# mLSTM cell and tanh-shrink MLP on one core: partial sums added in DRAM, one early unit fewer, explicit places for the later units

## The chip, the cores and the metric

The kernel runs on one core of a Trainium2 chip. The metric is the device time of one execution in microseconds (us), as the median of several runs. The engines are PE (matrix products), DVE and ACT (elementwise work, ACT also activations), POOL and SP (both used here mostly to issue DMAs). PSUM is written by PE and read by DVE and ACT; eight banks of it are shared out by tags.

## The reference

An mLSTM cell over 4 batches, 8 heads, 768 steps and a head size of 40 gives x, and an MLP without bias follows:

```python
for t in range(S):
    m_new = np.maximum(f_gate[:, :, t] + m, i_gate[:, :, t])
    f_stab = np.exp(f_gate[:, :, t] + m - m_new)
    i_stab = np.exp(i_gate[:, :, t] - m_new)
    C = f_stab * C + i_stab * np.einsum('bhd,bhe->bhde', vt, kt)
    n = f_stab * n + i_stab * kt
    y[:, :, t] = sigmoid(o_gate[:, :, t]) * (C @ qt) / np.maximum(np.abs(n @ qt), 1.0)
x = y.transpose(0, 2, 1, 3).reshape(3072, 320)
h = x @ w_in                  # 320 x 2048
g = h - np.tanh(h)
out = g @ w_out               # 2048 x 320
```

(m is carried along, and broadcasts are left out.) All is float32.

## The kernel before, in words

**Units and groups.** The cell is computed in chunks of 128 steps. A unit is one chunk of one batch with all its heads: 24 units, n = 4 x chunk + batch, so unit n needs the state that unit n - 4 left. Two units make a group of 256 tokens for the MLP: 12 groups. The 2048 hidden columns are eight pairs of 128-column blocks. The work of a group with a pair is an up product (x by w_in, tiles ph_up), g from a polynomial (z, q on ACT, gt on DVE) and a down product (gt by w_out).

**A unit.** Loads of k, v, o and of k and q turned (kz, qz). The scores ps = q k, then P (ps by the mask of decays, on DVE or by ACT and POOL), vs (v scaled), the products of P with vs and of the old state with q (ph), then the gate: den, o and ys, which is y. The update of the state is pc. The turn of y to x (px, xT) lets the up product read it.

**Two forms of a unit.** The units below PLANNED belong to the first part: ph has the tokens on the partitions, and y is turned by PE. The later units are turned through DRAM. Their products give pT with the head's dimensions on the partitions (`block_turned`); `turn_back` writes zt with DVE and sends it by SP as h_rows and back as z_in; `gate_turned` makes den, o and two ys of it in four steps; `turn_by_store` turns ys to yt on DVE, sends it by SP as y_rows, and reads it back as xT. SP's queue is served in order. All of one unit's zt legs and y legs go through it.

**Items.** The MLP is worked off in 49 items, each a pair of (group, pair). The table `RUNS` sets the first 11: they hold groups 0 to 3 with pairs 0 to 3, and group 0 with pairs 4 to 7. Their down products for pairs 0 to 3 run plainly into a bank po of each unit, and where a run of pairs ends (`evict`), po goes into an SBUF tile `part`: the first time by a copy on ACT, after that by an add on DVE. START is the twelfth item, from which on the dense part runs: 38 items with split up products (x_thirds, w_thirds) and a down product in seven multiplications (pS), for which DVE makes the sums s. `put_together` combines the banks of a group on DVE and, for groups 0 to 3, adds `part`; POOL sends the result.

**What sets the order.** In the first part a list scheduler, `Plan`, takes the step that can start first, by engine times written into the code, and among equal ones by rank; it fills waits of PE with products whose result is unused (awake). In the dense part the code's own order is the order on each engine. An item lists its PE steps with costs, and `merge` puts other steps among them by their place within the item. `cell_slot` places the steps of two units into a slot of two items: begin of unit s and the load of unit s + 1 (by POOL) at its start, `prepare` (vs) a fifth of the way, and the four gate steps and the store of unit s - 1 in its last quarter. The unit's scores ps stand in the item where it begins and `block_turned` in the one behind.

Of the kernel before, what the change touches and what calls it, by code (L numbers as in the profile page):

```python
# [61 lines left out]
L = 128  # L62
# [26 lines left out]
def kernel(  # L89
# [76 lines left out]
    class Plan:  # L166
# [14 lines left out]

        def add(self, engine, us, step, after=(), rank=0.0, take=(), give=(), at=0.0, kb=0.0, tiles=1, hold=0.0, dense=1.0, lag=None, small=False):
# [122 lines left out]
    FIRST, SPLIT, PLANNED, TAIL = 4, 4, 9, 1  # L305
# [71 lines left out]
    def load_unit(n, names=("kz", "qz", "v", "k", "o", "q2"), queue=SP, behind=(), crossed=False):  # L377
# [3 lines left out]
        for name in names:  # L381
# [3 lines left out]
            elif name in ("kz", "qz"):  # L385
                t[name] = load.tile([128, HH, L], FP, name=name, tag=f"{name}{(n + 1) % 3 if n < PLANNED and not general else n % 2}", bufs=1)
# [568 lines left out]
    def cell_slot(s, o):  # L955


        steps, pause = [], [(0.0, lambda: None)]
        if s is not None:
            if s + 1 < NU and s + 1 not in ld:  # L960
                load_unit(s + 1, ("kz", "qz", "v", "k", "o"), G, crossed=True)
            begin(s)
        if o is None:
            return [(0.0, lambda: prepare(s))]
        steps += 5 * pause
        if s is not None:
            steps.append((0.0, lambda: prepare(s)))
        steps += 8 * pause
        gates = []
        steps.append((0.0, lambda: [gates.extend(gate_turned(o)), gates[0]()]))  # L970
        steps += [(0.0, lambda i=i: gates[i]()) for i in range(1, 4)]
        steps.append((0.0, lambda: turn_by_store(o)))
        return steps + 2 * pause


# [77 lines left out]

    def put_together(g, halves_of=False):
# [14 lines left out]
        def end():  # L1069
            V.tensor_tensor(out=ob[:, 1:3], in0=bank[2], in1=u, op=OP.add)  # L1070
            if g < FIRST:
                both = ob[:, 0:2 * GT]
                V.tensor_tensor(out=both, in0=both, in1=parts_of[g].rearrange("p t (two n) -> p (t two) n", two=2), op=OP.add)
            c, b = divmod(g * GT, B)
            rows = out.rearrange("(b c t) n -> c t b n", b=B, c=NT)[c][:, b:b + GT]
            Clock.later("sent", 2.0, lambda: G.dma_start(out=rows, in_=ob[:, 0:4].rearrange("p (t two) n -> p t (two n)", two=2)))
# [273 lines left out]
    def down(x, some, g, p, first, last, evict_at_once=True):  # L1350
# [10 lines left out]
        def evict(tt):  # L1361
            n = g * GT + tt
            if last < NP - 1:
                if first:
                    V.tensor_tensor(out=part[n], in0=po[tt], in1=part[n], op=OP.add)
                else:
                    A.copy(out=part[n], in_=po[tt])
                return
            ob = mlp.tile([128, 5, HM], FP, name="ob", tag="ob")[:, 0:2].rearrange("p two n -> p (two n)")
            if first:  # L1370
                V.tensor_tensor(out=ob, in0=po[tt], in1=part[n], op=OP.add)
            else:
                A.copy(out=ob, in_=po[tt])
            send(n, ob, 1.0)
# [42 lines left out]
    RANKS = (-1.0, -1.0, -8.2006, -8.4463, 6.0242, 2.3893, 9.5327, 2.6415, 25.6922, 13.6176, 29.7021, 7.061)  # L1417
    WEIGHTS = (0.08, -0.3563, 5.1266, 7.6972, 9.6586, 11.6503, 11.1391, 25.4848)
# [7 lines left out]
    def gates(c0, c1, rank, at, banks_of, after=()):  # L1426
# [3 lines left out]
        for step in gate_rows(c0, c1):  # L1430
            op = plan.add("V", 0.2 + long, step, [op] if op else [*after, *rows[-1:]], rank, at=at)
# [5 lines left out]
        def add(engine, us, name, after, take=None, give=None):  # L1437
# [6 lines left out]
            op = plan.add(engine, us, step, after, rank, dense=0.2, take=[(names[take], mine)] if take is not None else (), give=[(names[give[0]], mine)] if give else ())  # L1444
# [27 lines left out]
    def plan_gates(i, rank, at, banks_of):  # L1472
        c0, c1 = CHUNKS[i:i + 2]
        after = [plan.add("S", 1.6, lambda: load_gates(c0, c1), (), rank - 0.5, at=at - 4.0, kb=33 * (c1 - c0))] if c0 > 1 else []
# [7 lines left out]
    def plan_unit(n, rank):  # L1482
# [7 lines left out]
        def load(name, us, kb, after):  # L1490
            u[name] = plan.add("S", us, lambda: [load_unit(n, (name,), behind=[T.last] if n == 2 and name == "kz" else ()), arrive(n)], of(*after) + of(n - 1, name), rank + LATE.get(name, 0.0) + 2.0 * (n < 2), at=6.0 + 8.0 * (n < 2), kb=kb, small=name == "q2")
# [27 lines left out]
        u["scores"] = plan.add("T", 1.0, first_part, [u["qz"], *(of(n - 2, "second") if n in (2, 3) else [])], rank, [(bank, held), ("P", held)], tiles=2, hold=HOLD * (n // B), dense=0.4 if n else 0.6)  # L1519
        if n in BY_POOL:  # L1520
            copies = [plan.add("A", 0.55, lambda i=i: ready[1][i][0](), [u["scores"]], rank - 6.4275, give=[(bank, held)] if i else ()) for i in range(2)]
            u["mask"] = [plan.add("G", 0.9, lambda i=i: ready[1][i][1](), [copies[i]], rank + 2.098, lag=0.1) for i in range(2)]
        else:
            u["mask"] = [plan.add("V", 0.62, lambda i=i: ready[1][i](), [u["scores"]], rank - 1.673, give=[(bank, held)] if i else ())
# [3 lines left out]
        u["prep"] = plan.add("V" if alone else "A", 0.45 if alone else 1.9, lambda: prepare(n, whole=False, by_heads=not alone), [u["v"], u["scores"], *of_tokens[c]], rank, [("vs", held)])  # L1528
        u["column"] = plan.add("A", 0.2, lambda: un[n]["column"](), [u["prep"]], rank - 0.2)
        u["open"] = plan.add("A", 0.47 if n else 1.75, lambda: open_gate(n), [u["o"], u["column"] if n < 2 else u["scores"], *of_states[0], *exponentials], rank - 0.1)  # L1530
# [9 lines left out]
        for j, heads in enumerate(parts):  # L1540
            op = plan.add("T", 0.223 * len(heads) + (0.22 if c else 0.0), lambda j=j, heads=heads: second_part(j, heads),
# [3 lines left out]
        if shared:  # L1545
            steps = []
            over = plan.add("V", 0.6, lambda: [steps.extend(gate(n, in_parts=True)), steps[0]()], [op], rank - 0.2851)
            shares = plan.add("A", 1.9, lambda: steps[1](), [over, u["open"]], rank + 9.0221)
            u["gate"] = plan.add("V", 0.5, lambda: steps[2](), [shares, *of(n - 2, "turn")], rank - 7.2476, give=[("small", held)])
        else:  # L1550
            u["gate"] = plan.add("V", 1.6, lambda: gate(n), [op, u["open"], *of(n - 2, "turn")], rank, give=[("small", held)])
# [13 lines left out]
        u["turn"] = plan.add("T", 0.35, turns, [u["gate"]], rank, [("small", held_x)], dense=0.5)  # L1565
        u["x"] = plan.add("A", 0.5, lambda: keep_x(n), [u["turn"]], rank + 1.345, give=[("small", held_x)])
        late = rank + (3.0653 if c else -10.0273)
        u["update"] = plan.add("T", 0.64, updates, [u["second"], u["k"]], late, [("small", held_c)], [("vs", held)],
                               at=0.0 if c else 0.0 if n < 2 else 50.4842, dense=0.5)
        u["state"] = plan.add("V", 1.0 if c else 0.5, lambda: keep_state(n), [u["update"], *before, *of_states[c]], late, give=[("small", held_c)])  # L1570
# [3 lines left out]
    def plan_weights(p, rank, at):  # L1574
        for k, block in enumerate(blocks_of(p)):
            fetch, parts, low, power, one, sign, product = block
            held, r, buffer = {}, rank + 4.428 * k, "w64" + "ab"[k]
            op = plan.add("G", 0.6 if k else 2.2, lambda fetch=fetch: fetch(begun[-1:]), begun_in_plan[:], r, [(buffer, held)], at=FETCH.get((p, k), at), kb=655)
            op = plan.add("V", 0.8, parts, [op], r, [("w", held)])
            if p == k == 0:  # L1580
                first_parts.append(op)
            two = [plan.add("A", 0.74, step, [op], r) for step in (low, power)]
            op = plan.add("V", 0.75, one, two[:1], r)
            op = plan.add("V", 0.75, sign, [op, two[1]], r, give=[(buffer, held)])
            converted[p, k] = plan.add("V", 0.75, product, [op] + (of_tokens[NT - 1] + of_states[NT - 1] if p >= KEPT and k == 1 else []), r, give=[("w", held)])
# [3 lines left out]
    for n in range(2):  # L1589
        plan_unit(n, -1.0)  # L1590
    plan_weights(0, 0.08, 3.4)
    begun_in_plan[:] = first_parts
    for n in range(2, PLANNED):
        if n == 2 * B:
# [15 lines left out]
    def plan_item(x):  # L1610
# [17 lines left out]
        for k in range(2 * n):  # L1628
            op = plan.add("T", 0.87, lambda k=k: products(k), [op] if op else [*need, *firsts[-1:]], rank, () if op else [("up", held)])
# [7 lines left out]
        op = ups[x] = plan.add("T", 0.43 * n, rest, [op], rank, tiles=2, dense=0.7)  # L1637
# [398 lines left out]
```

## Time and profile before

| what | us |
|---|---|
| runs | 491.85, 491.89, 496.38; median 491.89 |
| profiled execution | 492.65, span 490.9 |
| first dense product on PE | 139.72 |
| DVE busy, PE busy | 405.9 (83%), 476.0 (97%) |
| ACT busy, POOL busy | 256.8 (52%), 125.1 (25%) |

The span is what the profiler sees between the first and last instruction; the rest of the time is around it. In the rows below, a line shows start or group, engine, operation, the tile that it writes, the tiles that it reads, and shapes. Nearly all instructions carry the line of a helper (L115 or L138), so they are told apart by tile names. A bracket at the end shows how long the engine was idle before, and what ended that.

### The profile page before, as it was taken

Reading aid. Unit: us, or ns where it says so; the run is one execution under the profiler, and the core shown is the slowest. Engines: PE = TensorE matmul, PEld = TensorE weight load, DVE = VectorE, ACT = ScalarE, POOL = GpSimd, SP = SyncE. Lnnn points to the kernel's source line nnn. Section 1 sums busy time; section 2 is a strip of 40 time slices with the busy share of each in tenths; the row PEclk is TensorE's granted clock in tenths of the full one; section 3 lists DMA queues with packets and bytes.
Section 4 is the critical chain, followed back from the end, with each engine's and each line's share of the span. In section 5 each row is a group of like instructions: output and inputs, shape, how many; then the busy total and the mean of one; then the engine's idle time right before and its main releaser. Section 6 shows DMA issues by size and latency. Waiting matters only on the chain.

```text
span 490.9 us, 12662 instructions
## 1 busy us (share of the span) xinstructions
PE 476.0 (97%) x4783; PEld 426.6 (87%) x4783; DVE 405.9 (83%) x918; ACT 256.8 (52%) x600; POOL 125.1 (25%) x230
## 2 busy tenths in 40 slices
PE   8999999999999998999999999999999999999994
PEld 5778888777789898889999999999999999999994
DVE  5999969999979999997996896986888878775643
ACT  4566597765375656434544445445345454455450
POOL 4523304352003250532442351342143000000000
PEclk9999999999999999999999999999999999999999
DMA  7988737341001443535444454454454532320001
GB/s 222 294 257 257 194 66 133 116 140 44 1 1 58 83 103 70 146 88 120 107 104 106 108 125 83 108 119 83 90 124 89 95 77 41 64 60 1 28 1 33
DMA packets 122625, 49.57 MB, mean 101 GB/s; under 512 B 102806, under 2 KB 114710, under 8 KB 122558
## 3 DMA queue, kind: packets, MB, share of 16 engines
q1 hardware_dynamic: 112390, 23.12, 23.7%
q0 software_dynamic: 9968, 25.25, 17.1%
q8 instruction: 40, 0.66, 0.6%
q10 hardware_dynamic: 200, 0.33, 0.2%
q14 instruction: 27, 0.22, 0.2%
HBM read 37.57 MB, written 10.81 MB: 99 GB/s over the span
## 4 chain that ended last, share of the span: by engine, by line
PE 80%; DVE 11%; DMA 4%; issue 2%; ACT 1%; POOL 1%; SPq 0%; DVEq 0%
PE ph_up L138 34%; PE pS L138 26%; PE po L138 7%; PE ph L138 3%; DVE gt L115 3%; PE ps L138 3%; PE pT L138 3%; DMA w<-in_moe_w_in 2%; PE pc L138 2%; DVE s L115 2%; DVE w_thirds L115 1%; DVE zt L115 1%; DVE x_thirds L115 1%; DVE ob L115 1%; DMA h_rows<-zt 1%
## 5 line engine op out<-in xcount | busy, mean ns | idle before, releaser
L115 ACT ACTIVATE z<-ph_up 128x512 f32<-128x512 f32 (+1 forms) x98 | 56.8, 584 | 96.1 <-PE ph_up L138 96.1
L115 ACT ACTIVATE ph_up<-ph_up 128x512 f32<-128x512 f32 x76 | 44.2, 582 | 87.0 <-PE ph_up L138 83.4
L115 DVE SCALAR_TENSOR_TENSOR gt<-ph_up,z 128x512 f32<-128x512 f32 (+1 forms) x98 | 62.8, 673 | 23.4 <-ACT z L115 23.1
L138 PE MATMUL pS<-wT,s 128*128 128x160 f32 x480 | 72.0, 299 | 0.2 <-DVE s L115 0.2
L138 PEld LDWEIGHTS pS<-wT,s 128*128 128x128 f32 x480 | 67.3, 190 | 0.6 <-DVE s L115 0.4
L115 ACT ACTIVATE q<-z,tiny 128x512 f32<-128x512 f32 (+1 forms) x98 | 65.5, 711 | 0.6
L115 DVE SCALAR_TENSOR_TENSOR gt<-q,gt 128x512 f32<-128x512 f32 (+1 forms) x98 | 63.2, 673 | 0.0
L115 POOL DMA_DIRECT2D out<-ob x11 | 8.0, 726 | 208.7 <-DVE ob L115 129.4
L138 PE MATMUL pS<-w_out,gt 128*128 128x160 f32 x320 | 58.6, 312 | 0.0
L138 PE MATMUL ph_up<-x_thirds,w_high 128*128 128x256 f32 x304 | 52.0, 293 | 4.1 <-DVE gt L115 4.1
L138 PE MATMUL ph_up<-xT,w_half 64*64 64x256 f32 (+1 forms) x624 | 53.5, 392 | 0.0
L138 PEld LDWEIGHTS pS<-w_out,gt 128*128 128x128 f32 x320 | 45.5, 189 | 4.8 <-issue 3.0
L138 PE MATMUL ph_up<-x_thirds,w_thirds 128*128 128x256 f32 x304 | 48.4, 281 | 0.6 <-DVE x_thirds L115 0.6
L138 PEld LDWEIGHTS ph_up<-x_thirds,w_high 128*128 128x128 f32 x304 | 41.6, 188 | 5.1 <-issue 3.7
L138 PE MATMUL ph_up<-thirds,w_thirds 128*128 128x256 f32 x280 | 44.1, 292 | 0.4 <-ACT ph_up L115 0.4
L138 PEld LDWEIGHTS ph_up<-x_thirds,w_thirds 128*128 128x128 f32 x304 | 41.2, 188 | 0.8 <-DVE x_thirds L115 0.8
L138 PEld LDWEIGHTS ph_up<-xT,w_half 64*64 64x64 f32 (+1 forms) x624 | 27.7, 144 | 12.7 <-issue 3.0
L138 PE MATMUL ph_up<-xT,w_in 128*128 128x256 f32 x160 | 38.3, 383 | 0.0
L138 PE MATMUL po<-w_out,gt 128*128 128x320 f32 x128 | 38.0, 441 | 0.0
L138 PEld LDWEIGHTS ph_up<-thirds,w_thirds 128*128 128x128 f32 x280 | 37.1, 189 | 0.8 <-ACT ph_up L115 0.8
L138 PEld LDWEIGHTS ph_up<-xT,w_in 128*128 128x128 f32 x160 | 29.5, 190 | 4.3
L138 PEld LDWEIGHTS po<-w_out,gt 128*128 128x128 f32 x128 | 23.2, 190 | 9.6 <-issue 0.8
(143 smaller groups left out, 862.5 us busy)
## 6 DMA issues: line engine op xcount, KB each, us to landing
w<-in_moe_w_out POOLq DMA_DIRECT2D x8, 640.0 KB, 5.8
w<-in_moe_w_in POOLq DMA_DIRECT2D x16, 256.0 KB, 4.7
h_rows<-zt SPq DMA_DIRECT2D x60, 64.0 KB
z_in<-h_rows SPq DMA_DIRECT2D x60, 64.0 KB
out<-ob POOLq DMA_DIRECT2D x11, 320.0 KB, 2.8
y_rows<-yt SPq DMA_DIRECT2D x60, 48.0 KB
xT<-y_rows SPq DMA_DIRECT2D x30, 96.0 KB
kz<-in_kT POOLq DMA_DIRECT2D x28, 80.0 KB, 2.7
```

The source lines that it names most:

```text
L115: i = method(*args, **kwargs)
L138: return cls.keep(nc.tensor.matmul(*args, **kwargs))
```

## The change

It has four parts.

1. **Parts added in DRAM.** The DVE adds into `part` and the add of `part` in `put_together` are gone. Each run's po is copied by ACT into `part` and sent by POOL to `out` (`send_group`): the first send of a group stores, every later one, that of `put_together` among them, is a DMA that adds to what lies there, with a dependency on the group's send before it. Ten such stores stand in the first part, four plain and six adding.
2. **One planned unit fewer.** PLANNED goes from 9 to 8, so unit 8 is computed in the dense form. Units 8 and 9 are both loaded by SP ahead of START.
3. **Explicit places.** `cell_slot` is gone. Unit n begins at item START + max(0, 2(n - 8) - 1); its `prepare` stands 0.45 items on, the load of unit n + 2 (by POOL) 1.7 on, the four gate steps 2.7 to 2.97 and the store 3.06 on.
4. **New order of the first part.** Every step of the plan has a name, and a table `SHIFTS` adds a number to the rank of each name; the ranks of units and weights are new too.

```diff
+        SHIFTS = {"update": -76.14, "g": -103.12, "x": 41.17, "column": 70.86, "turn": -207.65, "shared": -147.21,
...
+            rank, self.name = rank + self.SHIFTS.get(self.name, 0.0), None
...
-    FIRST, SPLIT, PLANNED, TAIL = 4, 4, 9, 1
+    FIRST, SPLIT, PLANNED, TAIL = 4, 4, 8, 1
...
+    def send_group(g, tile):
+        c, b = divmod(g * GT, B)
+        rows = out.rearrange("(b c t) n -> c t b n", b=B, c=NT)[c][:, b:b + GT]
+        i = G.dma_start(out=rows, in_=tile, **({"accum_op": OP.add} if g in stored else {}))
+        if g in stored:
+            tc.add_manual_dep(i.ins, stored[g].ins.name, SYNC, reason="order of additions")
+        stored[g] = i
...
             V.tensor_tensor(out=ob[:, 1:3], in0=bank[2], in1=u, op=OP.add)
-            if g < FIRST:
-                both = ob[:, 0:2 * GT]
-                V.tensor_tensor(out=both, in0=both, in1=parts_of[g].rearrange("p t (two n) -> p (t two) n", two=2), op=OP.add)
...
-                if first:
-                    V.tensor_tensor(out=part[n], in0=po[tt], in1=part[n], op=OP.add)
-                else:
-                    A.copy(out=part[n], in_=po[tt])
+                A.copy(out=part[n], in_=po[tt])
...
-    slots = [tuple(n if PLANNED <= n < NU else None for n in (s, s - 1)) for s in range(PLANNED, NU + 1)]
-    last = item((NG - 1) * NP) - 2.0
-    for i, slot in enumerate(slots):
-        x0, x1 = (START + (last - START) * j / len(slots) for j in (i, i + 1))
-        begins[int(x0)].append((slot, x0, x1))
+    def place(at, step):
+        work[int(at)].append((at, 0.0, step))
+
+    def gate_at(n, at):
+        gates = []
+        place(at, lambda: [gates.extend(gate_turned(n)), gates[0]()])
+        for i in range(1, 4):
+            place(at + 0.09 * i, lambda i=i: gates[i]())
+        place(at + 0.36, lambda: turn_by_store(n))
+
+    EACH = ("kz", "qz", "v", "k", "o")
+    for n in range(PLANNED, NU):
+        at = START + max(0, 2 * (n - PLANNED) - 1)
+        begins[at].append(n)
+        place(at + 0.45 * (n > PLANNED), lambda n=n: prepare(n))
+        if n + 2 < NU:
+            place(at + 1.7, lambda n=n: load_unit(n + 2, EACH, G, crossed=True))
+        gate_at(n, at + 2.7)
```

**The order on DVE in one dense period.** The rows run from the end of den (the reciprocal) to yt and what follows. Names: gt<-ph_up and gt<-q are the two steps of g, each for half an item; ys is y by its low and high dimensions; yt its turn for the store; zt belongs to the next unit; s are the sums for the down products. Before:

```order
L115 RECIPROCAL den<-den 128x8
L115 TENSOR_TENSOR o<-o,den 128x320
L115 SCALAR_TENSOR_TENSOR gt<-ph_up,z 128x512 x2
L115 TENSOR_TENSOR ys_156<-z_in,o 128x8x32
L115 TENSOR_TENSOR ys_156<-z_in,o 128x8x8
L115 STREAM_TRANSPOSE yt<-ys_156 128x256
L115 STREAM_TRANSPOSE yt<-ys_156 128x128
L115 TENSOR_TENSOR thirds<-x_thirds 128x768
L115 SCALAR_TENSOR_TENSOR gt<-q,gt 128x512
L115 STREAM_TRANSPOSE zt<-pT 128x64
```

and in the changed kernel:

```order
L115 RECIPROCAL den<-den 128x8
L115 SCALAR_TENSOR_TENSOR gt<-ph_up,z 128x512
L115 TENSOR_TENSOR o<-o,den 128x320
L115 SCALAR_TENSOR_TENSOR gt<-ph_up,z 128x512
L115 TENSOR_TENSOR ys_157<-z_in,o 128x8x32
L115 SCALAR_TENSOR_TENSOR gt<-q,gt 128x512
L115 TENSOR_TENSOR ys_157<-z_in,o 128x8x8
L115 SCALAR_TENSOR_TENSOR gt<-q,gt 128x512
L115 TENSOR_TENSOR s_3215<-gt 128x256 x2
L115 TENSOR_TENSOR s_3216<-s_3215,gt 128x256
L115 TENSOR_TENSOR s_3217<-gt,s_3216 128x256
L115 STREAM_TRANSPOSE yt<-ys_157 128x256
```

den now stands ahead of the first gt<-ph_up of an item instead of the next one's beginning, and between it and yt the whole of an item's g and sums has moved in; in every second unit thirds stands between the two ys.

**The order on POOL in the first part.** w are the fetches of weights (w_in in four pieces, w_out in one), P the masked scores that POOL makes, out the stores. Before, in the middle of the first part:

```order
L115 AFFINE_SELECT P<-P 128x512 x2
L115 DMA w_690<-in_moe_w_in 128x256
L115 DMA w_690<-in_moe_w_in 128x2x128
L115 DMA w_690<-in_moe_w_in 64x128 x2
L115 DMA w_774<-in_moe_w_in 128x256
L115 DMA w_774<-in_moe_w_in 128x2x128
L115 DMA w_774<-in_moe_w_in 64x128 x2
L115 AFFINE_SELECT P<-P 128x512 x2
L115 DMA w_951<-in_moe_w_out 128x2x320
```

and in the changed kernel:

```order
L115 DMA out<-part 128x2x320
L115 DMA w_714<-in_moe_w_out 128x2x320
L115 AFFINE_SELECT P<-P 128x512 x2
L115 DMA w_796<-in_moe_w_in 128x256
L115 DMA w_796<-in_moe_w_in 128x2x128
L115 DMA w_796<-in_moe_w_in 64x128 x2
L115 DMA out<-part 128x2x320 x2
L115 DMA w_881<-in_moe_w_out 128x2x320
```

Stores of parts now stand between the fetches: five of the ten ahead of the last fetch, five behind it. PE's rows ahead of START keep their counts except for unit 8's (ps 72 to 64, ph<-vs,P 72 to 64, ph<-state 10 and 5 to 8 and 4, pc 18 and 9 to 16 and 8, px 27 to 24) and awake (42 to 39). On ACT the last copy of po stands behind the first x_thirds of the dense part.

More of the change, by code (lines that the diff above doesn't have):

```diff
@@ L180, in __init__, with of @@
             self.tiles, self.done = 1, []
+        def of(self, name):
+            self.name = name
+            return self
+        name = None
+        SHIFTS = {"update": -76.14, "g": -103.12, "x": 41.17, "column": 70.86, "turn": -207.65, "shared": -147.21,
+                  "g_load": -260.96, "store": 132.5, "split": 51.35, "open": 92.01, "state": 54.14, "x_up": -14.25,
+                  "cube": -104.02, "fetch": 221.34, "evict": -174.94, "sums_g": -102.61, "parts": 88.45, "z": -27.79,
+                  "q": 67.28, "product": -162.48, "up": -125.33, "sums_w": 39.35, "seven": 113.81, "over": 90.23,
+                  "gates": -99.77, "pool_mask": 113.85, "mask": -9.78, "loads": 84.62, "two": 160.52, "down": 87.24,
+                  "second": -26.64, "x_cross": -316.14, "g_rows": 204.49, "sign": -118.98, "one": -105.4, "scores": -344.38,
+                  "copy": -55.99, "gate": -17.9, "x_low": -187.13, "rest": 27.76, "prep": -282.1, "share": -195.25}
         def add(self, engine, us, step, after=(), rank=0.0, take=(), give=(), at=0.0, kb=0.0, tiles=1, hold=0.0, dense=1.0, lag=None, small=False):
             self.serial += 1
+            rank, self.name = rank + self.SHIFTS.get(self.name, 0.0), None
             op = {"engine": engine, "us": us, "step": step, "after": list(after), "rank": rank, "serial": self.serial,
@@ L953, in gate_turned @@
         return [over, share, lambda: product(0), lambda: product(1)]
[L955 to L973, printed above, removed]
     gT, po = {}, {}
@@ L1430, in gates @@
         for step in gate_rows(c0, c1):
-            op = plan.add("V", 0.2 + long, step, [op] if op else [*after, *rows[-1:]], rank, at=at)
+            op = plan.of("g_rows").add("V", 0.2 + long, step, [op] if op else [*after, *rows[-1:]], rank, at=at)
         rows.append(op)
@@ L1442, in step @@
                 steps[name]()
-            op = plan.add(engine, us, step, after, rank, dense=0.2, take=[(names[take], mine)] if take is not None else (), give=[(names[give[0]], mine)] if give else ())
+            op = plan.of("gates").add(engine, us, step, after, rank, dense=0.2, take=[(names[take], mine)] if take is not None else (), give=[(names[give[0]], mine)] if give else ())
             return op if take is None else (op, (take, mine))
@@ L1768 @@
         G.memset(tile[:, H:], 0.0)
-    load_unit(PLANNED, ("kz", "qz", "v", "k", "o"), crossed=True)
+    for n in (PLANNED, PLANNED + 1):
+        load_unit(n, EACH, crossed=True)
     FIRST_B = [(PLANNED + i) % B for i in range(B)]
@@ L1787 @@
         dense, new, scored = [], [], news
-        for slot, x0, x1 in begins[x]:
-            spread_over(cell_slot(*slot), x0, x1)
-            if slot[0] is not None:
-                new.append(slot[0])
+        for n in begins[x]:
+            begin(n)
+            new.append(n)
         if x < len(items):
```

101 lines of the change are left out of this document (52 added, 49 removed).

## The prediction

> **What bounds the kernel now.** I read the table of stages first, to see which engine is full in which part, then the DVE and SP timelines of one dense period, then the waits, then the groups that the change adds and removes. The profiled execution took 492.65 us with a span of 490.9, so 1.75 us lie around the span; it is 0.76 above the median of 491.89, and every sum below is made against 492.65 and brought to the median at the end. The stages are cut at the first dense product (139.72) and at two item starts (212.48, 426.35). Columns: stretch, its length, then busy time of PE, PE weight load, DVE, ACT, POOL, clock, DMA share, GB/s.
>
> ```profile
> 20.00:139.72 119.72, 118.85 (x729) 96.33 (x728) 108.36 (x226) 78.97 (x189) 32.31 (x61) 1.00 0.50 135
> 139.72:212.48 72.76, 67.18 (x815) 62.03 (x815) 68.91 (x161) 39.23 (x95) 20.63 (x37) 1.00 0.36 81
> 212.48:426.35 213.87, 213.87 (x2682) 202.59 (x2682) 177.73 (x414) 103.29 (x239) 58.64 (x104) 1.00 0.45 98
> 426.35:490.90 64.55, 57.81 (x434) 53.56 (x433) 36.46 (x80) 25.67 (x58) 1.46 (x2) 0.99 0.09 24
> ```
>
> The first part is PE's (118.85 of 119.72 us), the early dense stretch DVE's (68.91 of 72.76), the long stretch PE's again with no idle time, at a granted clock of 1.00. By engine totals a change that takes work from DVE should do no harm. But a period of the long stretch also holds a round trip through DRAM for each unit, which no busy time shows. DVE's part of one period, in the order in which it ran:
>
> ```profile
> 286.41 0.16 DVE L115 SCALAR_TENSOR_TENSOR den<-z_in,inv 128x8 f32<-128x8 f32 x1
> 287.05 0.49 DVE L115 TENSOR_TENSOR o<-o,den 128x320 f32<-128x320 f32 x1
> 287.60 1.29 DVE L115 SCALAR_TENSOR_TENSOR gt<-ph_up,z 128x512 f32<-128x512 f32 x2
> 288.81 0.55 DVE L115 TENSOR_TENSOR ys<-z_in,o 128x256 f32<-128x256 f32 x2
> 289.39 0.64 DVE L115 STREAM_TRANSPOSE yt<-ys 128x256 f32<-128x256 f32 x2
> 291.24 0.65 DVE L115 STREAM_TRANSPOSE zt<-zt 128x448 f32<-128x448 f32 x1
> 292.98 0.75 DVE L115 TENSOR_TENSOR s<-gt 128x256 f32<-128x256 f32 x2
> 294.64 0.48 DVE L115 TENSOR_TENSOR vs<-v,crossed 128x320 f32<-128x320 f32 x1
> 299.21 1.28 DVE L115 SCALAR_TENSOR_TENSOR gt<-q,gt 128x512 f32<-128x512 f32 x2
> 305.72 0.17 DVE L115 SCALAR_TENSOR_TENSOR den<-z_in,inv 128x8 f32<-128x8 f32 x1 [1.55 <-DMA z_in<-h_rows]
> 309.12 0.92 DVE L115 TENSOR_TENSOR thirds<-x_thirds 128x768 fp32r<-128x768 f32 x1
> ```
>
> SP's queue beside it, between the first and the last unit of the stretch (the time of a row is that of issuing; a queue's next row waits for the landing it needs):
>
> ```profile
> 200.29 1.86 SPq L115 DMA_DIRECT2D y_rows<-yt  x4
> ...
> 209.30 1.90 SPq L115 DMA_DIRECT2D z_in<-h_rows  x4
> ...
> 290.06 2.46 SPq L115 DMA_DIRECT2D y_rows<-yt  x4
> 295.25 1.24 SPq L115 DMA_DIRECT2D xT<-y_rows  x2
> 296.59 2.18 SPq L115 DMA_DIRECT2D h_rows<-zt  x4
> 300.95 1.90 SPq L115 DMA_DIRECT2D z_in<-h_rows  x4
> ...
> 414.78 1.85 SPq L115 DMA_DIRECT2D y_rows<-yt  x4
> ...
> 423.13 1.90 SPq L115 DMA_DIRECT2D z_in<-h_rows  x4
> ```
>
> Read the two together as a ring. den(n) opens the gate of unit n and ends with yt(n), 3.62 us later (286.41 to 290.03). Only then SP sends y_rows(n); xT stands behind it and waits for its landing; h_rows(n+1) stands behind xT though its source zt was ready at 291.89; z_in(n+1) waits for h_rows; and den(n+1) needs z_in. That den ran at 305.72 after waiting 1.55 us for exactly this. The gap from the y_rows to the z_in issue has a mean of 9.74 us over the 13 units between 200.29 and 423.13 (9.01 for the first, 8.35 for the last, and 10.89, the longest, for the one of the DVE rows). From z_in's issue to den it is 4.21 on average over the eight units whose den waited (4.77 above). The DRAM part is thus 13.95, the ring 3.62 + 13.95 = 17.6.
>
> ```profile
> 195.85 0.16 DVE L115 SCALAR_TENSOR_TENSOR den<-z_in,inv 128x8 f32<-128x8 f32 x1
> ...
> 427.85 0.17 DVE L115 SCALAR_TENSOR_TENSOR den<-z_in,inv 128x8 f32<-128x8 f32 x1 [1.13 <-DMA z_in<-h_rows]
> ...
> DVE den L115 <- DMA z_in<-h_rows: 6.9, 8, 1.6
> ...
> PE ph_up L138 <- DVE gt L115: 4.1, 3, 1.8
> ```
>
> From den(10) at 195.85 to den(23) at 427.85 there are 13 passes in 232.0 us, 17.85 each. PE needs 18.08 for two items with a unit (rows below), so the ring and PE are level: eight dens waited, 6.9 us in all, and PE hardly felt it.
>
> ```profile
> 291.12 0.74 PE L138 MATMUL ph_up<-x_thirds,w_high 128*128 128x256 f32 x4
> ...
> 299.66 0.74 PE L138 MATMUL ph_up<-x_thirds,w_high 128*128 128x256 f32 x4
> ...
> 309.20 0.74 PE L138 MATMUL ph_up<-x_thirds,w_high 128*128 128x256 f32 x4
> ```
>
> **Explicit places (the large term).** The gate moves from +3.33 items after a begin to +2.7, and its steps are laid 0.09 of an item apart with the store of yt last, at +0.36. In the new DVE order shown ahead, den now stands before both gt<-ph_up of the item, and between den and yt stand two gt<-ph_up, o, ys, two gt<-q and the four sums s; before, it was o, two gt<-ph_up and ys. In prices of the rows above: den 0.64 (286.41 to 287.05), gt<-ph_up 2 x 0.60 (287.60 to 288.81), o 0.55, ys 0.58, gt<-q 2 x 0.64, s 1.66 (292.98 to 294.64), yt 0.64: 6.55, by the starts that overlap some 0.2 less, 6.35. In every second unit thirds (0.83) stands there too, half of it on average: 6.75. DVE has nothing to skip these with. It is idle 36 us in 214, but it runs in order, and after a den that waited everything behind it is ready.
>
> SP's order is unchanged: y_rows, xT, h_rows of the next unit, z_in. So the ring becomes 6.75 + 13.95 = 20.70 us, above PE's 18.08. What is late next is den, by about 2.6 us in every period; behind it wait both gt<-ph_up of that item, and the ph_up banks they free are those that the next item's first products write. The 13 passes cost 13 x 20.70 = 269.1; the last two carry no loads of later units and take the shortest DRAM part, 8.35 + 4.72 = 13.07, so 1.8 less: 267.3. Against 232.0 that is **+35.3**.
>
> The bounds: with 13.07 in every pass the ring is 19.82 and the term +25.7; with 15.66 (290.06 to 305.72, the slowest) it is 22.4, +59. I take the mean, since the loads now issued at +1.7 items fall into the same part of the ring as before.
>
> The Trainium skill ("DMA: Bandwidth & Descriptors", section "Anatomy of one DMA — SWDGE (gpsimd) path") gives a transfer a fixed 2.0 us and 436 GB/s beside it. Four legs in a row, of 192, 192, 256 and 256 KB here, would by that be an estimated 10.1 us, and the ring an estimated 16.9, below PE's 18.08. The trace disagrees: it measured 13.95, and that fit is for POOL's queue while these are SP's.
>
> **First part: the stores, unit 8, the new ranks.**
>
> ```profile
> L138 PE MATMUL ps<-qz,kz 40*64 40x128 f32 (+2 forms) x624 | 22.9, 251 | 0.0
> ...
> L138 PE MATMUL ph<-vs,P 128*128 128x41 f32 x144 | 18.1, 274 | 0.4 <-POOL P L115 0.4
> ...
> L138 PE MATMUL pc<-vs,k 128*64 128x41 f32 (+2 forms) x230 | 14.6, 241 | 0.0
> ...
> L138 PE MATMUL awake<-diag 128*128 128x512 bf16 x42 | 12.2, 427 | 1.1 <-DVE probe L115 1.1
> ...
> L138 PE MATMUL ph<-state,q 120*128 120x123 f32 (+1 forms) x30 | 6.0, 283 | 0.0
> ...
> L142 PE MATMUL px<-ident,ys 128*128 128x128 f32 x27 | 4.4, 278 | 0.0
> ...
> L115 DVE TENSOR_TENSOR part<-po,part 128x320 f32<-128x320 f32 x12 | 5.7, 485 | 1.9 <-PE po L138 1.8
> ...
> L115 DVE TENSOR_TENSOR ob<-ob,part 128x640 f32<-128x640 f32 x4 | 3.3, 825 | 0.1
> ...
> L115 POOL DMA_DIRECT2D out<-ob x11 | 8.0, 726 | 208.7 <-DVE ob L115 129.4 <-DVE den L115 79.4
> ```
>
> With unit 8 go from PE's first part: ps 22.9/24 = 0.95, ph<-vs,P 18.1/9 = 2.01, ph<-state 6.0/5 = 1.20, pc 14.6/20 = 0.73 (the last four units have none), the turn of x 3 x 4.4/27 = 0.49, and three awake fillers at 12.2/42 = 0.29 each: **-6.3**. All other PE counts stay. DVE loses there twelve adds of parts (12 x 0.485 = 5.8), but PE is the fuller engine, so that only widens DVE's slack and is worth nothing by itself. ACT gains twelve copies, some 5 us of the 40 it has idle in that stage. POOL gains ten stores at 0.73 us of issue, between its weight fetches. New waits stand against this: a store waits on POOL for its part's copy, and an accumulating one for the group's earlier store, with weight fetches behind it; and the last copy of po1 stands behind an x_thirds on ACT. Cover: POOL sits idle 87 of 119.72 us there, mostly for buffers. Bounds 0 and +6 (all of the relief); I take +2. START moves by **-4**, to about 135.7. What the new ranks do beyond the counts I cost at nothing, since PE has 0.9 us of idle time there to win and can lose as much as it is made to wait, inside the same +6.
>
> **Early dense stretch.** DVE bounds it. Before den(10) it now has one more z block (zt 1.4, state 0.6), one more gate (den, o, ys, yt 2.2), less two adds of parts (2 x 0.82), and a first wait of about 1: **+3.4** on the 56.13 us from 139.72 to 195.85. Unit 8's PE work fits in the 5.6 us that PE is idle there. The other two adds lie in this stretch or behind den(10), under the ring. The loads of units 8 and 9 stand on SP ahead of START and are hidden by the first part.
>
> **Tail.** den(23) stood 1.5 us into an item (427.85 against 426.35) with 8 items to come in 64.55 us, 8.07 each. Now it stands some 1.3 us before an item's end, with seven after it: 1.3 + 56.5 = 57.8 against 63.05, **-5.2**.
>
> **Sum:** -4 + 3.4 + 35.3 - 5.2 = +29.5; 492.65 + 29.5 = 522.1, and less 0.76 about **521 us** for the median.
>
> **The rivals.** (a) The ring does not bind: the DRAM part comes down to 11.3 us or less, so that den is on time. Then the passes take PE's 18.08, 13 x 0.23 = +3.0, and the sum is -4 + 3.4 + 3.0 - 5.2 = -2.8: 489, not slower. It decides where y_rows-issue to den falls by 2.6 us. The fit of the Trainium skill's page "DMA: Bandwidth & Descriptors" above speaks for it. Against it: the last unit, the shortest of the 13 by its first gap and without loads beside it, still took 13.07. (b) xT's wait is no longer in the way, and only the z trip binds: den to the freed banks 1.24, one item with a unit 9.54 (299.66 to 309.20), at whose end zt now stands, and h_rows' issue to den 9.13 (296.59 to 305.72): 19.9, 13 x 19.9 - 232.0 = +26.7 for the passes, and with the rest as above 513. SP's order, where xT stays ahead, speaks against it. (c) The chain binds and the accumulating stores also hold POOL and the weights behind them: START +4 instead of -4, 529. POOL's idle time speaks against it. (d) The first part shrinks by DVE's whole relief of about 11 us and the dense stretch loses nothing: -11 + 3.4 + 3 - 5.2 = -9.8, 482; PE's full stage speaks against it.
>
> **How the numbers follow.** The forecast has 0.60, (b) 0.13, (c) 0.08, (a) 0.13, (d) 0.06. The measurement of this kernel tells about 1% from no change, so (a) at 489 counts as the same, (d) as faster, the rest as slower: 0.06, 0.13, 0.81. The range: the ring with the shortest DRAM part gives 521 - 9.6 = 511, rival (b) 513, and if only half of the lengthening from 3.62 to 6.75 came, the ring would be 19.1 and the time about 503; toward (a) I reach to 499, and upward past (c) to 533. Outside are (a), (d) and the slowest legs in every pass.
>
> **What would show it.** Right: in the new profile den waits for z_in in nearly every period, 2 us or more each, dens stand 19.8 to 21 us apart, den to yt is 6.3 to 7.2 us, and PE waits for gt with a total of 25 to 40 us; START is at 133 to 139. Wrong: dens 18.1 apart with little wait (then (a)); yt soon after den; POOL's fetches late in the first part ((c)). The step that would fail first is that y_rows, xT, h_rows and z_in keep their 13.95 us when the ring turns more slowly and its transfers meet others.

## The result and the profile after

The changed kernel takes 546.77 us at the median against 492.04 in the same runs: a ratio of 1.107, interval 1.099 to 1.114. The direction was as forecast, the size was not: +54.7 us instead of +29, and the time lies above the range of 499 to 533. The profiled execution took 549.84 us with a span of 548.0.

The windows view of the changed kernel, cut at the same four events as in the prediction's sum (the first dense product, den(10), den(23)). Columns as before: stretch, length, busy time of PE, PE weight load, DVE, ACT, POOL, then the granted clock, DMA share, GB/s.

```profile
20.00:133.46 113.46, 113.34 (x678) 91.10 (x676) 106.74 (x211) 77.80 (x190) 34.22 (x60) 1.00 0.66 162
133.46:198.72 65.26, 58.49 (x722) 54.21 (x721) 53.96 (x131) 33.55 (x80) 23.48 (x39) 0.95 0.45 87
198.72:483.89 285.17, 247.41 (x2912) 232.33 (x2912) 192.47 (x453) 112.49 (x258) 65.41 (x114) 0.95 0.39 82
483.89:548.00 64.11, 54.64 (x398) 50.98 (x398) 35.60 (x77) 23.13 (x51) 0.71 (x1) 0.94 0.07 18
```

No engine is full in the long stretch now: PE is busy 247 of 285 us, DVE 192, and PE's granted clock has gone from 1.00 to 0.95. Against the kernel before, by stage:

| stage | before | after | difference | forecast |
|---|---|---|---|---|
| to the first dense product (START) | 139.72 | 133.46 | -6.3 | -4 |
| START to den(10) | 56.13 | 65.26 | +9.1 | +3.4 |
| 13 passes, den(10) to den(23) | 232.00 | 285.17 | +53.2 | +35.3 |
| den(23) to the end | 63.05 | 64.11 | +1.1 | -5.2 |
| span | 490.9 | 548.0 | +57.1 | +29.5 |

The waits view of the changed kernel names the place: engine, what waited, for whom, total us, times, longest.

```profile
DVE den L115 <- DMA z_in<-h_rows: 47.2, 15, 5.8
...
PE ph_up L138 <- DVE gt L115: 40.8, 14, 4.2
```

den waits in 15 of 16 units, 47.2 us against 6.9 before, and PE waits behind it for gt, 40.8 us against 4.1. One period, from the timelines of DVE, PE and SP:

```profile
356.48 0.17 DVE L115 SCALAR_TENSOR_TENSOR den<-z_in,inv 128x8 f32<-128x8 f32 x1 [3.24 <-DMA z_in<-h_rows]
...
357.96 0.68 DVE L115 SCALAR_TENSOR_TENSOR gt<-ph_up,z 128x512 f32<-128x512 f32 x1
...
361.89 0.63 DVE L115 STREAM_TRANSPOSE yt<-ys 128x256 f32<-128x256 f32 x2
...
366.67 0.65 DVE L115 STREAM_TRANSPOSE zt<-zt 128x448 f32<-128x448 f32 x1
...
377.64 0.17 DVE L115 SCALAR_TENSOR_TENSOR den<-z_in,inv 128x8 f32<-128x8 f32 x1 [3.07 <-DMA z_in<-h_rows]
```

```profile
357.79 0.71 PE L138 MATMUL ph_up<-x_thirds,w_high 128*128 128x256 f32 x4 [3.13 <-DVE gt L115]
...
378.95 0.70 PE L138 MATMUL ph_up<-x_thirds,w_high 128*128 128x256 f32 x4 [2.79 <-DVE gt L115]
```

```profile
362.55 3.01 SPq L115 DMA_DIRECT2D y_rows<-yt  x4
368.15 1.24 SPq L115 DMA_DIRECT2D xT<-y_rows  x2
369.48 2.18 SPq L115 DMA_DIRECT2D h_rows<-zt  x4
373.15 2.28 SPq L115 DMA_DIRECT2D z_in<-h_rows  x4
```

Two rings share den here. The **y ring** is the forecast's: den, g and s, yt, y_rows, xT, then h_rows and z_in of the next unit, den: 6.07 us on DVE to the y_rows issue (356.48 to 362.55) and 15.1 in the queue (362.55 to 377.64), 21.2 in all. The **z ring** goes another way: den, gt<-ph_up, PE's next item (it starts at 357.79, 1.31 after den), the turn pT in that item, zt (ends 367.32, 9.53 after the start), h_rows, z_in, den. Without a wait for xT it would take 1.31 + 9.53 + 8.16 (369.48 to 377.64) = 19.0 here. Over the 13 passes, legs from the first (198.72) to the last (483.89) in the timelines: den to the y_rows issue 6.62 (before 3.72), from there to den 15.32 (before 14.13), 21.94 together. In three of the 13, h_rows left within 0.03 us of zt's end, so there the z ring came last; in the other ten the y ring did.

What makes the z ring longer than 19 in six of the 13 passes is PE's clock; the three passes in which it came last are among them, and in the other three h_rows still waited for xT. Two windows of 8 us of the changed kernel, each from the start of the item behind such a wait:

```profile
357.79:365.79 8.00, 8.00 (x120) 7.50 (x121) 6.53 (x16) 3.82 (x9) 2.00 (x4) 1.00 0.15 31
378.95:386.95 8.00, 8.00 (x100) 7.54 (x100) 5.78 (x14) 2.20 (x5) 0.38 (x1) 0.79 0.12 18
```

In the same 8 us, PE ran 120 products at a granted clock of 1.00 and 100 at 0.79. From the item's start to zt it takes 11.05 to 12.51 us in those six passes and 9.51 to 9.53 in the other seven.

Of two experiments below, e4 and e8, the profiled executions were longer than their medians by 10 and 11 us, with START 11 and 15 us later than in the kernels that they edit, so only the passes and the order are read from them.

### The profile page after: what moved, and what is told of

Same layout as the page of the kernel before. It is cut to its first block, busy times and chain, and to the rows that moved or that the text cites. A ratio compares the mean times of both kernels' runs of the same rounds, so it can differ in the third digit from the quotient of the medians.

```text
span 548.0 us, 12833 instructions
## 1 busy us (share of the span) xinstructions
PE 492.5 (90%) x4837; PEld 441.3 (81%) x4837; DVE 402.8 (74%) x911; ACT 256.9 (47%) x602; POOL 135.7 (25%) x238
## 4 chain that ended last, share of the span: by engine, by line
PE 44%; DVE 20%; DMA 18%; SPq 9%; issue 4%; ACT 4%; DVEq 0%; ACTq 0%
PE ph_up L138 19%; PE pS L138 10%; SPq L115 9%; DMA z_in<-h_rows 9%; PE po L138 6%; DMA h_rows<-zt 6%; DVE gt L115 6%; DVE s L115 4%; PE ph L138 3%; DVE zt L115 3%; DMA y_rows<-yt 3%; PE ps L138 2%; DVE den L115 2%; ACT q L115 2%; PE awake L138 1%
## 5 line engine op out<-in xcount | busy, mean ns | idle before, releaser
L138 PE MATMUL ph_up<-x_thirds,w_high 128*128 128x256 f32 x304 | 56.0, 309 | 40.8 <-DVE gt L115 40.8
L138 PEld LDWEIGHTS ph_up<-x_thirds,w_high 128*128 128x128 f32 x304 | 44.5, 203 | 44.0 <-issue 40.5
L138 PEld LDWEIGHTS pS<-wT,s 128*128 128x128 f32 x480 | 69.0, 194 | 0.1
L138 PE MATMUL pS<-w_out,gt 128*128 128x160 f32 x320 | 63.0, 329 | 3.2 <-DVE ob L115 3.2
L138 PEld LDWEIGHTS pS<-w_out,gt 128*128 128x128 f32 x320 | 49.5, 203 | 7.6 <-issue 5.6
L138 PE MATMUL ph_up<-x_thirds,w_thirds 128*128 128x256 f32 x304 | 52.4, 298 | 0.0
L115 POOL DMA_DIRECT2D qz<-in_qT x28 | 14.4, 518 | 131.6 <-PE pT L138 131.4
L138 PEld LDWEIGHTS ph_up<-x_thirds,w_thirds 128*128 128x128 f32 x304 | 45.1, 205 | 0.0
L115 POOL DMA_DIRECT2D out<-ob x11 | 10.0, 907 | 124.3 <-DVE ob L115 117.8
L115 DVE SCALAR_TENSOR_TENSOR den<-z_in,inv 128x8 f32<-128x8 f32 x16 | 2.7, 167 | 47.2 <-DMA z_in<-h_rows 47.2
```

The source lines that it names most:

```text
L115: i = method(*args, **kwargs)
L138: return cls.keep(nc.tensor.matmul(*args, **kwargs))
```

## The experiments

All times are medians; "before" was run beside each set (492.73, 495.62 and 492.20 us). The stages of their profiled executions, cut at the same events:

| run | us | ratio, interval | START | to den(10) | 13 passes | tail |
|---|---|---|---|---|---|---|
| e1, begin earlier, gate 3.36 | 497.38 | 1.009 (1.007 to 1.012) | 133.36 | 64.85 | 233.21 | 64.18 |
| e2, stores and ranks alone | 499.47 | 1.014 (1.009 to 1.020) | 145.57 | 53.56 | 234.74 | 64.63 |
| e3, gate steps at one place | 571.52 | 1.154 (1.145 to 1.163) | 137.38 | 73.73 | 292.33 | 66.86 |
| e4, before, gate behind den 0.34 later | 498.37 | 1.010 (1.008 to 1.013) | | | 232.70 | |
| e5, as e3, gate at 2.85 | 500.43 | 1.014 (1.007 to 1.020) | 134.05 | 62.41 | 241.20 | 60.54 |
| e6, y on POOL's queue | 534.57 | 1.084 (1.074 to 1.095) | 133.45 | 65.45 | 275.22 | 59.38 |
| e7, e1 with DVE adds | 496.88 | 1.006 (1.003 to 1.010) | 133.81 | 66.27 | 232.97 | 62.15 |
| e8, loads later | 552.46 | 1.115 (1.103 to 1.126) | | | 281.53 | |
| e9, before with the places alone | 556.54 | 1.133 (1.126 to 1.139) | 139.88 | 61.23 | 283.97 | 62.92 |
| e10, e1 and e7, steps at one place | 498.25 | 1.014 (1.008 to 1.020) | 133.87 | 66.31 | 232.17 | 63.95 |

START itself moved between 133.4 and 137.4 us over kernels with the same first part (after, e1, e3, e5, e6); smaller differences there say nothing.

### Which part costs the time: e1, e2, e9

e1 is the changed kernel with another phase:

```diff
-        at = START + max(0, 2 * (n - PLANNED) - 1)
+        at = START + max(0, 2 * (n - PLANNED) - 2)
-        place(at + 0.45 * (n > PLANNED), lambda n=n: prepare(n))
+        place(at + 0.55 * (n > PLANNED), lambda n=n: prepare(n))
-            place(at + 1.7, lambda n=n: load_unit(n + 2, EACH, G, crossed=True))
+            place(at + 2.7 - (n == PLANNED), lambda n=n: load_unit(n + 2, EACH, G, crossed=True))
-        gate_at(n, at + 2.7)
+        gate_at(n, at + (3.36 if n > PLANNED else 2.02))
```

> The changed kernel with units begun one item earlier (item START + 2(n - 9) from unit 9 on) and the gate 3.36 items behind the begin, so that the gate stands in the same item as the turn of the next unit, as before; stores in DRAM, eight planned units and the new ranks stay. Theory (the ring of den, yt, y_rows, xT, h_rows, z_in): den to yt falls to about 2.3 us, the ring to 16.5 to 17.7, under PE's 18.08; the 13 passes take about 235 us instead of 285 and the time is 485 to 497 us. Rival (the stores that add in DRAM, or the new order of the first part, cost the time): it stays above 530 us.

e2 puts the old slots, nine planned units and their loads back into the changed kernel:

```diff
-    FIRST, SPLIT, PLANNED, TAIL = 4, 4, 8, 1
+    FIRST, SPLIT, PLANNED, TAIL = 4, 4, 9, 1
...
-    for n in range(PLANNED, NU):
-        at = START + max(0, 2 * (n - PLANNED) - 1)
...
-        gate_at(n, at + 2.7)
+    slots = [tuple(n if PLANNED <= n < NU else None for n in (s, s - 1)) for s in range(PLANNED, NU + 1)]
...
+        begins[int(x0)].append((slot, x0, x1))
```

> Only the stores in DRAM and the new ranks; nine planned units and the old slots (parts 2 and 3 of the change undone). Theory of the ring: passes of 17.8 to 18.2 us as before, time 485 to 494 us. Rival (stores or ranks cost the time): above 530 us.

e9 is the kernel before with the explicit places in the room of its slots, nothing else:

```diff
-        begins[int(x0)].append((slot, x0, x1))
+    for n in range(PLANNED, NU):
+        at = START + 2 * (n - PLANNED) + (n > PLANNED)
+        begins[at].append(n)
+        place(at + 0.45 * (n > PLANNED), lambda n=n: prepare(n))
+        if n + 1 < NU:
+            place(at, lambda n=n: load_unit(n + 1, EACH, G, crossed=True))
+        gate_at(n, at + 2.7)
```

> The kernel before with nothing but the explicit places: unit n begins one item later than before (START + 2(n - 9) + 1 from unit 10 on), prepare 0.45 and the gate 2.7 to 3.06 items behind the begin; nine planned units, DVE adds and ranks as before. Theory of the two rings: DVE's order is that of the changed kernel, den ahead of gt<-ph_up and the turn of the next unit an item later, so passes of 21 to 23 us instead of 17.85, granted clock down behind the longer waits of PE, time 533 to 558 us. Rival (the slowdown needs the stores, the lost planned unit or the ranks too): below 515 us.

The places alone give 556.5 us, as much as the whole change and a little more, with passes of 283.97 us; the same waits stand in its profile:

```profile
DVE den L115 <- DMA z_in<-h_rows: 46.1, 14, 5.3
PE ph_up L138 <- DVE gt L115: 44.1, 16, 5.2
```

With another phase and everything else of the change, e1 has 497.4 us, 0.4 above its range, and passes of 233.21. So the places of part 3 are enough for the loss, and with the old slots (e2) or another phase (e1) it is gone. e2's time missed its expectation by 5.5 us at the top: its passes were right (18.06 us each), but START came at 145.57 instead of 139.72. Whether the stores do that or ranks that belong to eight units isn't told apart by it.

### Which ring: e3, e5, e6

e3 shortens only the y ring, by laying the gate's steps at one place:

```diff
-            place(at + 0.09 * i, lambda i=i: gates[i]())
-        place(at + 0.36, lambda: turn_by_store(n))
+            place(at, lambda i=i: gates[i]())
+        place(at, lambda: turn_by_store(n))
```

> The changed kernel, the four gate steps and the store of yt laid at one place (2.7 items on) instead of 0.09 apart: den to yt 2.3 us instead of 6.6. If the ring through y_rows and xT is the only one: 2.3 + 15.3 = 17.6, below PE's 18.08, time 490 to 500 us. If the shorter ring of z (den, both gt<-ph_up, the next item's products, zt, h_rows, z_in) is next in line: 2.9 + 9.5 + 8.2 to 8.7 = 20.6 to 21.1 per pass, time 530 to 537 us.

It got worse than the change itself, 571.5 us, above both of its ranges. den to the y_rows issue is 2.43 us as wanted. A period of e3 on DVE, and the same one on SP:

```profile
375.33 0.17 DVE L115 SCALAR_TENSOR_TENSOR den<-z_in,inv 128x8 f32<-128x8 f32 x1 [3.11 <-DMA z_in<-h_rows]
377.09 0.64 DVE L115 STREAM_TRANSPOSE yt<-ys 128x256 f32<-128x256 f32 x2
377.65 1.25 DVE L115 SCALAR_TENSOR_TENSOR gt<-ph_up,z 128x512 f32<-128x512 f32 x2
...
388.81 0.65 DVE L115 STREAM_TRANSPOSE zt<-zt 128x448 f32<-128x448 f32 x1
397.52 0.17 DVE L115 SCALAR_TENSOR_TENSOR den<-z_in,inv 128x8 f32<-128x8 f32 x1 [1.06 <-DMA z_in<-h_rows]
```

```profile
377.75 1.86 SPq L115 DMA_DIRECT2D y_rows<-yt  x4
381.02 1.24 SPq L115 DMA_DIRECT2D xT<-y_rows  x2
389.48 1.96 SPq L115 DMA_DIRECT2D h_rows<-zt  x4
```

xT is out of the way at 382.3, but h_rows leaves only at 389.48, with zt. The whole z ring can be read here: PE starts at 378.45, 3.12 after den, since yt now stands ahead of gt<-ph_up; zt ends 11.01 later, at a clock of 0.79; h_rows to den takes 8.04: 22.2 us. The expectation had 20.6 to 21.1, without the clock. PE's waits, up to 5.6 us, bring the clock down in seven of the 13 passes.

e5 differs from e3 by one number, the gate's place, 2.85 instead of 2.7 items on. On DVE den then stands behind both gt<-ph_up of its item:

```diff
-        gate_at(n, at + 2.7)
+        gate_at(n, at + 2.85)
```

> As the run with the gate steps at one place (571.5 us), but at 2.85 items instead of 2.7: on DVE den, o, ys, yt then stand behind both gt<-ph_up of the item instead of ahead of them; nothing else differs. Theory now: what cost 571.5 us is the ring den, gt<-ph_up, PE's next item, zt, h_rows, z_in, den, made longer by PE's lower granted clock behind each wait; with den behind gt<-ph_up PE is out of that ring, and the y ring is 2.4 + 14 to 15.3 = 16.4 to 17.7, so PE's 18.08 bound it: passes 235 to 240 us, time 492 to 502 us. Rival (any gate in the item where the next unit begins is too early for z_in): over 530 us.

```profile
365.67 1.28 DVE L115 SCALAR_TENSOR_TENSOR gt<-ph_up,z 128x512 f32<-128x512 f32 x2
366.87 0.16 DVE L115 SCALAR_TENSOR_TENSOR den<-z_in,inv 128x8 f32<-128x8 f32 x1
...
368.63 0.64 DVE L115 STREAM_TRANSPOSE yt<-ys 128x256 f32<-128x256 f32 x2
```

The time falls from 571.5 to 500.4 us by having two instructions of 0.64 us ahead of den. The z ring is cut, since PE no longer waits for den: its waits for gt fall from 56.0 us in e3 to 2.5. Passes are 241.20 / 13 = 18.55 us, a little over PE's 18.08.

In e1 den stands ahead of gt<-ph_up too, and no z ring costs time there: the next unit is turned on PE in the same item, ahead of what den holds up, instead of the item behind. In one pass of e1 zt ended at 351.82 and den came at 362.64, so 10.8 us lay between them where h_rows and z_in need some 8.7. It is the two together, den ahead of the banks' release and the next unit's turn behind it, that close the ring.

e6 cuts the other ring, by moving y_rows and xT from SP's queue to POOL's:

```diff
-            SP.dma_start(out=rows[:, part].rearrange("(b i) j -> i b j", i=BLOCK), in_=yt[part])
+            G.dma_start(out=rows[:, part].rearrange("(b i) j -> i b j", i=BLOCK), in_=yt[part])
...
-            SP.dma_start(out=x_tile(g)[half, :, tt * L:(tt + 1) * L], in_=rows.rearrange("(c p) t -> p c t", p=128)[half])
+            G.dma_start(out=x_tile(g)[half, :, tt * L:(tt + 1) * L], in_=rows.rearrange("(c p) t -> p c t", p=128)[half])
```

> The changed kernel with y_rows and xT on POOL's queue instead of SP's, so that h_rows no longer stands behind xT; den stays ahead of gt<-ph_up. If the ring through y_rows is all: it is gone, passes 18.1 us, 490 to 500 us. If the ring of z stands right behind it: 1.3 + 9.5 + 8.2 to 9.7 = 19 to 20.5 per pass, 247 to 267 us for 13, time 509 to 529 us.

The y ring is gone, h_rows leaves 0.02 us behind zt in every pass, and the passes still take 275.22 / 13 = 21.17 us. Its legs, as means of the 13: 1.31 from den to PE's start, 10.28 to zt, 4.72 to the z_in issue, 4.83 to den. The expectation had 19 to 20.5; what it lacked is the clock (four of the 13 items ran at 0.61 to 0.79 and took 11.0 to 12.3 us to zt) and the two DMA legs, 0.3 and 0.45 us longer than in the kernel before. So the two rings were nearly equally long in the changed kernel: cutting the y ring alone saves 0.8 us per pass, shortening it alone saves nothing, and e5, which cuts the z ring with the y ring short, brings PE back as the bound, as e1's phase does. Cutting the z ring with the y ring left long was not run.

### What is no cause: e4, e7, e8

e4 is the kernel before with three of the four gate steps and the store of yt 0.34 of an item later. A slot has 21 steps, counted from 0; the first gate step, den, is step 14, so the edit leaves it where it was and moves what follows it:

```diff
-            at = x0 + i * (x1 - x0) / len(steps)
+            at = x0 + i * (x1 - x0) / len(steps) + 0.34 * (i >= 15)
```

> The kernel before with one edit: the gate steps and the store of yt 0.34 of an item later; nothing else of the change. In its order both gt<-ph_up, one gt<-q, zt and the sums then stand between den and yt, about 8 us instead of 3.7. Theory of the ring: 8 + 14 to 15.3 = 22 to 23.3 per pass, 13 passes cost 54 to 71 us more, time 545 to 565 us. Rival (the gate's place alone does not matter): 490 to 496 us.

This expectation failed: 498.4 us. DVE's order is as it said, but zt of the next unit then stands ahead of yt, and so SP's queue has its order turned:

```profile
378.53 1.96 SPq L115 DMA_DIRECT2D h_rows<-zt  x4
382.48 1.93 SPq L115 DMA_DIRECT2D z_in<-h_rows  x4
384.45 1.00 SPq L115 DMA_DIRECT2D y_rows<-yt  x2
```

With h_rows and z_in ahead of y_rows there is no y ring, and no den waits for z_in in its profile. Its passes take 232.70 us, as before. What its waits show besides is that x comes late:

```profile
ACT x_thirds L115 <- DMA xT<-y_rows: 24.6, 7, 4.5
```

Where the 6 us over the kernel before lie isn't told by a profile that is 10 us longer than the median. So the distance from den to yt is no cost to the passes by itself; it is one where h_rows stands behind xT in the queue.

e7 is e1 with the parts added by DVE again: the add in `evict`, the add in `put_together`, and no early stores.

```diff
-                A.copy(out=part[n], in_=po[tt])
+                if first:
+                    V.tensor_tensor(out=part[n], in0=po[tt], in1=part[n], op=OP.add)
+                else:
+                    A.copy(out=part[n], in_=po[tt])
...
+            if g < FIRST:
+                both = ob[:, 0:2 * GT]
+                V.tensor_tensor(out=both, in0=both, in1=parts_of[g].rearrange("p t (two n) -> p (t two) n", two=2), op=OP.add)
```

> The run with units begun one item earlier and the gate at 3.36 (497.4 us), with the parts added by DVE again (part 1 undone: no early stores, no adding DMA). If the stores cost in the first part: START earlier by 3 us or more and the time 490 to 494 us. If they are hidden and DVE's relief is worth nothing: within 2 us of 497.4; if the relief is worth something: 499 to 506 us.

496.88 against 497.38 us, with overlapping intervals and START at 133.81 against 133.36: the stores cost nothing that can be measured, and what DVE gains by them is worth nothing that can be measured. In the changed kernel the ten stores of the first part take a median of 4.8 us to land, while POOL is busy only 34 of the 113 us there.

e8 moves the loads of later units, which the changed kernel issues close to y_rows:

```diff
-            place(at + 1.7, lambda n=n: load_unit(n + 2, EACH, G, crossed=True))
+            place(at + 2.4, lambda n=n: load_unit(n + 2, EACH, G, crossed=True))
```

> The changed kernel with the loads of unit n + 2 at 2.4 items instead of 1.7. If the loads lengthen the y_rows leg (4.62 us in the changed kernel against 3.94 before): that leg falls to about 4 us and the passes by 0.6 us each, time 536 to 541 us. Rival (the loads do not matter, the ring is only longer because zt comes later and z_in's landing varies): 543 to 550 us.

552.5 us: no gain, and above both ranges. The mean gap from y_rows to xT is 4.7 us, against 4.6. The edit did not free that gap of POOL's transfers: its queue moves data there in nine of e8's 13 passes, in ten of the changed kernel's. But the kernel before, whose gap is 3.9, has them there in eleven, and more of them (0.32 MB a pass against 0.22). So transfers beside y_rows are not what tells the two kernels apart.

### A version better than both: e10

e10 is e7 with the gate's steps at one place, as in e3; there den and gt<-ph_up keep e1's phase.

> A try for a version that beats both: units begun one item earlier, gate at 3.36 with its steps at one place, parts added by DVE, eight planned units. The y ring is 2.4 + 14 = 16.4 and the z ring has an item's slack, so the passes stay PE's 18.0; what is left is the early stretch (65 us against 56 before) against START's 6 us: 493 to 498 us, no better than before.

498.25 us: the passes are PE's (17.86 us), den waits little, and the time is no better than before, as expected (0.25 above the range). No version here beats the kernel before. What e1, e7 and e10 win ahead of START (6 us) the early stretch takes back (9 to 10 us); there units 8 and 9 are begun in one item.

## Why the prediction was wrong

- **What bounds the kernel.** That the rings through DRAM and PE were level before, and that a longer ring would show as den waiting for z_in and PE for gt, was right: 47.2 and 40.8 us, the latter just above the 25 to 40 forecast.
- **"Explicit places (the large term)", +35.3, measured +53.2.** This is the step that failed. The DVE part of the y ring was right (6.75 forecast, 6.62 measured). "The ring becomes 6.75 + 13.95 = 20.70" took the DRAM part over unchanged; it measured 15.32, and 13 x 1.37 = 17.8 us is as much as the miss in this term. The prediction had named this as the step that would fail first, and its own upper bound for the term, +59 with the slowest DRAM part in every pass, covers the +53.2; the range left that out.
- **Where the 17.8 us lie.** 8.8 lie between the issues of y_rows and xT (4.62 us on average, before 3.94), 6.6 between z_in's issue and den (4.72, where the forecast took 4.21), and some 3 in passes where h_rows waited longer for zt, that is, for the z ring; from h_rows to z_in it was 0.7 less. The first isn't explained. In the second, POOL's store of a group and two loads of kz, 0.49 MB together, fall into the leg in four of the 13 passes, which take 5.69 us there on average; the other nine, with 0 to 0.41 MB, take 4.29. In the kernel before POOL's queue moves nothing in this leg in any pass. The DMA view of one of the four, from z_in's issue (217.47) to den (224.02), with queue, packets, MB and share of the 16 DMA engines (q0 carries POOL's DMAs, q1 SP's):

```profile
q0 software_dynamic: 368, 0.49, 48.3%
q1 hardware_dynamic: 2112, 0.26, 26.4%
```

No run changes this alone, so it isn't shown that these transfers lengthen the leg.
- **What (b) lacked.** The forecast took one ring as the bound and the other, (b), for a rival that excludes it, at 19.9 us. The two are nearly equally long: e6 measured the z ring at 21.17 with the y ring gone, and its time, 534.57, is not (b)'s 513. What (b) lacked is mainly that PE's waits behind den bring its granted clock down, so that the item in the z ring takes 11.1 to 12.5 us instead of 9.5 in six of the changed kernel's passes; the forecast had the clock at 1.00 throughout. In the changed kernel itself the z ring accounts for only the 3 us above; it decides once the y ring is shortened or cut, as in e3 and e6.
- **First part, -4, measured -6.3.** That is as much as the whole relief, without the +2 for new waits, and e7 shows that the stores are hidden. But START moved by 4 us between kernels with this first part, so a miss of 2 us says little. Rivals (c), START 4 us later, and (d), 11 us earlier with nothing lost behind it, are out.
- **Early stretch, +3.4, measured +9.1.** The forecast added DVE work and a wait of about 1 us. But den(8) waited 3.50 us for z_in, and 7.2 of the 9.1 us lie ahead of den(9), where PE is busy 38.45 us instead of 34.45, at a clock of 0.94. The other 1.9 lie between den(9) and den(10). The rings are not most of it: e1, e7 and e10, which have eight planned units and passes at PE's rate, take 64.9 to 66.3 us here, and e2 with nine 53.6; the new places with nine units (e9) take 61.2. So most of what leaves the first part with unit 8 seems to come back here.
- **Tail, -5.2, measured +1.1.** The working took 426.35 for an item's start, which it isn't. The items' starts around den(23) in PE's timeline, of the kernel before:

```profile
431.16 0.74 PE L138 MATMUL ph_up<-x_thirds,w_high 128*128 128x256 f32 x4
...
439.03 0.74 PE L138 MATMUL ph_up<-x_thirds,w_high 128*128 128x256 f32 x4
```

and of the changed one:

```profile
485.11 0.74 PE L138 MATMUL ph_up<-x_thirds,w_high 128*128 128x256 f32 x4 [3.23 <-DVE gt L115]
...
494.64 0.74 PE L138 MATMUL ph_up<-x_thirds,w_high 128*128 128x256 f32 x4
```

The next item starts 3.3 us behind den(23) (427.85) before and 1.2 behind it (483.89) after. That makes the term -2.1. The rest is that item, 9.53 against 7.87 us behind another wait of PE, and 1.5 us behind PE's last product (484.16 before, 539.75 after), from there to the end of the span, that nothing here explains.
- **Rival (a)**, that the ring does not bind, and the transfer times that spoke for it, are out: in the 13 passes the shortest DRAM part was 13.58 us, not 11.3.

## What to carry to other kernels

Before moving a step, list every cycle that returns to it a period later, through each engine's order and through each queue's, and take their maximum; e3 and e5 differ by the place of two DVE instructions and by 71 us. A step that may wait for a DMA belongs behind the instructions that free the matrix engine's banks, not ahead of them, unless the source of its next transfer comes out before them, as in e1 and in the kernel before. Last, a leg that is fed by PE must be priced with the clock that PE has after the waits one is about to add.

## What the runs showed of the hardware

The granted clock of PE fell after short waits. In the profiles of the changed kernel, e6 and e3 there are 42 waits of PE for gt<-ph_up in the 13 passes and just behind them, from 200.04, 200.21 and 214.24 us on. Behind the ten of 1.09 to 2.32 us the next 8 us ran at 1.00 each time. Of the 32 from 2.36 to 5.63 us, 19 were followed by 0.61 to 0.79, with no clear bound: 3.13 us at 357.79 kept 1.00 and 2.79 at 378.95 gave 0.79. The shortest that was followed by a fall, in e3's timeline of PE and the window behind it:

```profile
309.26 0.70 PE L138 MATMUL ph_up<-x_thirds,w_high 128*128 128x256 f32 x4 [2.36 <-DVE gt L115]
```

```profile
309.26:317.26 8.00, 8.00 (x102) 7.55 (x104) 4.43 (x9) 2.28 (x6) 0.46 (x1) 0.79 0.26 51
```

The Trainium skill, in "TensorE: Matmul & The Clock Gate", section "What's actually happening", says that the clock is halved after one idle window of about 3.4 us, and that the window runs freely. One such window at half speed would make 1 - 1.7/8 = 0.79 of 8 us, an estimate from that page's figure; 13 of the 19 falls have 0.79, the other six 0.61 to 0.70. That waits from 2.36 us on were enough differs from the same page's rule, in "HAM oscillation — how this bites in real kernels", that idle gaps over about 3.4 us are to be avoided; here the measurement decides.

A DMA that adds took longer than one that stores. The first four stores of `put_together` send 320 KB each; in e1 they add to what lies in `out`, in e7 they only store. The DMA views of e1 and e7 over these four (count, KB each, median us from issue to landing):

```profile
out<-ob POOLq DMA_DIRECT2D x4, 320.0 KB, 4.8
```

```profile
out<-ob POOLq DMA_DIRECT2D x4, 320.0 KB, 2.7
```

Issuing one took 1.17 to 1.25 us against 0.73. The times of e1 and e7 don't differ, so here this was hidden.
